# Attention into a MoE layer on one core: batches 3 and 4 turned by the DMA crossbar, attention planned one row chunk later, a fourth buffer of exponentials

## The chip, the cores and the metric

The kernel runs on one core of a Trainium2 chip. The metric is device time in microseconds (us), the median of the runs of a program. One execution of each kernel is profiled as well, and everything that is said of single instructions comes from that execution.

## The reference

```python
# q, k, v: [8 batches, 8 heads, 576 positions, 64] f32
scores = scale * np.matmul(q, k.transpose(0, 1, 3, 2))
scores = np.where(pos[:, None] // 64 >= pos[None, :] // 64, scores, -1e9)
attn = softmax(scores)                                   # over the keys
x = (attn @ v).transpose(0, 2, 1, 3).reshape(8 * 576, 8 * 64)     # 4608 x 512
h = x @ w_in                                             # 4608 x 2048
g = h * (1.0 / (1.0 + np.exp(-beta * h)))
out = g @ w_out                                          # 4608 x 512
```

The attention is causal in blocks of 64 positions. The kernel computes the matmuls in bf16 and gives f32.

## The kernel before

**Attention.** The work is cut into 32 pairs: for each of 8 batches four pairs of heads (u = 4 b + c). For a pair, Q and K are loaded by SyncE (SP), cast to bf16, and turned so that the head dimension lies on the partitions (QKT). In batches 0 and 1 TensorE (PE) turns them (line 561); from batch 2 on (QB = 2) the DMA crossbar does, two pairs at once (line 598). Four groups of score matmuls follow (QK, line 620; they use PE as two halves of 64 rows, one for each head), and for each group ScalarE (ACT) writes the exponentials (lines 628 and 640) into a buffer E; VectorE (DVE) zeroes the masked corners (634, 636). Then 30 matmuls (PV, line 664) multiply the exponentials with V, which carries a column of ones, so that the row sums come with it. DVE takes the reciprocals (676) and scales into xq (683). Last, xq is turned into xT, the transposed attention output: on PE by five transposes for a pair (line 708), copied out of PSUM by DVE or ACT (718, 716), in the batches below XB = 5; by the DMA crossbar from SP (line 696) in the batches from XB on. xT is a ring of 2560 columns; a batch whose 576 columns wrap around its end is moved in three pieces (`pieces`) instead of two, which of all batches is batch 4.

**MoE.** The 4608 rows are cut into 9 chunks of 512. For a chunk, 16 groups of four matmuls (line 752) give h, ACT takes a tanh of each (762), DVE forms the product gT (766), and 64 matmuls (line 785) multiply with w_out; ACT scales the result (797) and issues its store (803). Chunk r needs the attention of the batches that its rows lie in, batch r at the latest. gT has two buffers, one for even and one for odd chunks.

**Order.** All operations are first put into a planner (class `Plan`), which simulates the engines, the buffers and the two DMA rings with given durations, and at each step gives every engine its ready operation with the lowest `prio`. What it yields is the fixed order of every engine's queue; at run time each engine (and the queue of SP, which issues the loads and both kinds of crossbar transposes) goes through its list and waits on semaphores. The numbers that set the order around the change are these:

```python
        LAG = 2
        def pr(u):
            b, c = divmod(u, NPAIR)
            return u if b < 1 else 10 * u if b < 2 else 994 + 100 * (b - LAG) + 4.9 * c
```

QK of a pair has prio `pr(u) + .1` or `+ .2`, PV `pr(u) + .4`, the PE transposes `pr(u) + .5` (5 more for PV and transposes in batch 0), and the MoE of chunk r has `1000 + 100 * r + j` for its 16 groups of h and from `1016 + 100 * r` on for its products with w_out. Exponentials, tanh and most of DVE's work have 0, crossbar transposes -1, loads the number of their pair or batch. Until 50 us of the plan PE gets filling matmuls (469, 471) where it has nothing else.

**Buffers.** E has three buffers (NE = 3), which the pairs take in the order in which they come free. In batch 0 the scores don't wait for a buffer, only the exponentials do. xq has two buffers, QKT three, the raw Q and K six. PSUM has eight banks, of which scores take two pairs and PV one pair.

**Weights.** GpSimd (POOL) casts Q, K and V, and issues the loads of w_in and w_out, in four quarters each (lines 451 and 456). Quarter 1 of w_in has prio -33.2, the casts of V for pairs 2 and 3 of batch 0 have -33, quarters 2 and 3 have -32. Quarters 1 to 3 wait for all of batch 0's V, the w_out quarters for batch 1's V.

Of the kernel before, what the change touches and what calls it, by code (L numbers as in the profile page):

```python
# [4 lines left out]
ACT = mybir.ActivationFunctionType  # L5
ALU = mybir.AluOpType
f32 = mybir.dt.float32
bf16 = mybir.dt.bfloat16
# [7 lines left out]
RC = 512  # L16
NRC = NROWS // RC
NJ = NF // 128
# [320 lines left out]
def bass_blockwise_causal_attn__then__act_swish_beta_kernel(  # L339
# [10 lines left out]
    with es:  # L350
        def sb(name, shape, dt):
            return es.enter_context(nc.sbuf_tensor(name, shape, dt))

        NQ = 2
        QB, XB, CAST = 2, 5, "POOL"
        NE = 3
        NS = 6
        RX = 5 * RC
        ST = [sb(f"ST{i}", [128, 5, 4, 64], f32) for i in range(NS)]
        ST6 = [s[0:96].rearrange("p t h d -> p (t h d)")[:, 0:768].rearrange("p (h j d) -> p h j d", h=2, j=6)  # L360
               for s in ST]
        Vs = [sb(f"Vs{i}", [128, 5, 8, 64], f32) for i in range(NQ)]
        QKn = [sb(f"QKn{i}", [128, 2, 2, 768], bf16) for i in range(NQ)]
        Vn = [sb(f"Vn{i}", [128, 5, 8, 66], bf16) for i in range(NQ)]
        QKT = [sb(f"QKT{i}", [128, 2, 2, 640], bf16) for i in range(3)]
        Ef = [sb(f"E{i}", [128, 3200], bf16) for i in range(NE)]
        E3 = [e[:, 0:3072].rearrange("p (c h n) -> p c h n", c=3, h=2) for e in Ef]
        E4 = [e[:, 3072:3136] for e in Ef]
        inv = [sb(f"inv{i}", [128, 10], f32) for i in range(3)]
        xq = [sb(f"xq{i}", [128, 5, 128], bf16) for i in range(2)]  # L370
# [5 lines left out]
        betaT = sb("betaT", [NJ, 128], f32)  # L376
        beta = sb("beta", [128, NJ], f32)
        th = [sb(f"th{i}", [128, RC], f32) for i in range(3)]
        gT = [sb(f"gT{i}", [128, NJ, RC], bf16) for i in range(2)]
        ost = [sb(f"ost{i}", [128, DM], f32) for i in range(3)]  # L380
        warm = sb("warm", [128, 2], f32)
        PS = es.enter_context(nc.psum_tensor("PS", [128, 8, 512], f32))
# [2 lines left out]
        identW = identF[:].bitcast(bf16)  # L385
        NFILL, TFILL = 400, 50000.0
        P = Plan()
        for c, n in (("ST", NS), ("QKn", NQ), ("V", NQ), ("Vs", NQ), ("QKT", 3), ("E", NE), ("inv", 3), ("xq", 2),
                     ("th", 3), ("gT", 2), ("ost", 3)):
            P.slots(c, n)  # L390

# [6 lines left out]
        def dve_t(n):  # L398
            return (n + 125) / 0.96

        LAG = 2
        def pr(u):
            b, c = divmod(u, NPAIR)
            return u if b < 1 else 10 * u if b < 2 else 994 + 100 * (b - LAG) + 4.9 * c
# [16 lines left out]
        for i in range(NQ):  # L421
# [7 lines left out]
                ones.append(P.op("POOL", 100, mk(lambda g, i=i, h=h: g.memset(  # L429
                    Vn[i][64 * h:64 * h + 64, 4, h:8:2, 64:65], 1.0)), deps=[o], prio=-4))  # L430
            ones.append(P.op("POOL", 100, mk(lambda g, i=i: g.memset(Ef[i][:, 3136:3200], 0.0)), prio=-4))
        for i in range(NQ, NE):
            ones.append(P.op("POOL", 100, mk(lambda g, i=i: g.memset(Ef[i][:, 3136:3200], 0.0)), prio=-4))


# [1 line left out]
                  xfer=100, dma=("d_beta", 1), prio=0.1)  # L437
# [3 lines left out]
                  deps=[bt, c2], tiles=[tb], lat=400, mode="full", prio=5)  # L441
# [5 lines left out]
        win, wout = [], []  # L447
        for a in range(4):
            def fwi(g, e, a=a):
                n = slice(512 * a, 512 * a + 512)  # L450
                return [g.dma_start(w_in[:, :, n], moe_w_in[:, n].rearrange("(c p) n -> p c n", p=128))]

            win.append(P.op("POOL", 1000, fwi, xfer=3150, dma=(f"d_win{a}", 1), prio=-38.5 if a < 1 else -33.2 if a < 2 else -32))
        for a in range(4):
            def fwo(g, e, a=a):
                return [g.dma_start(w_out[:, 4 * a:4 * a + 4, :],
# [6 lines left out]
        for i in range(NFILL):  # L463
# [10 lines left out]
            n = 215 if i < 16 else 110  # L474
# [7 lines left out]
        for b in range(B):  # L482
            ts, t = P.tile("Vs"), P.tile("V")
            tl[b] = t
            for h0, h1 in ([(0, 4), (4, 8)] if b == 0 else [(0, 8)]):
                vs = []
                for i in range(6):
                    def fv(g, e, ts=ts, b=b, h0=h0, h1=h1, i=i):
                        if i < 4:
# [6 lines left out]
                    n = (h1 - h0) / 8 * (1 if i < 4 else 0.25)  # L496
                    vs.append(P.op("SP", 300 + 550 * n, fv, tiles=[ts],
                                   xfer=1580 * n, prio=3.5 + 0.1 * (h0 > 0) if b == 0 else 4 * b + (3.5 if b < 2 else 0.5),
                                   dma=["d_V", h0, 1]))
                ld["V", b, h0] = vs  # L500
                for g0 in range(h0, h1, 2 if b == 0 else 8):
                    g1 = g0 + 2 if b == 0 else h1

                    def fw(g, e, ts=ts, t=t, g0=g0, g1=g1):
# [3 lines left out]
                             prio=4 * b + 0.5 - (38.5 - 5 * (h0 > 0)) * (b < 1))  # L508
# [20 lines left out]
        for u in range(NU):  # L529
            b, c = divmod(u, NPAIR)  # L530
            Tv = tl[b]
            p = c % 2
# [5 lines left out]
            if b < QB:  # L538

                turned = []  # L540
                for w, (nm, src) in enumerate((("Q", q), ("K", k))):
# [9 lines left out]
                    def fn(g, e, ts=ts, tn=tn, p=p, w=w):  # L551
# [5 lines left out]
                             prio=-40 + 3 * u if onp else -1)  # L557

                    def ft(g, e, tn=tn, pt=pt, p=p, w=w):
                        for i in range(6):  # L560
# [5 lines left out]
                             prio=pr(u))  # L566
# [33 lines left out]

                turned = [P.op("SP", 3250, ft, deps=casts, tiles=[tt_, tn], xfer=3200, prio=-1, dma=["d_T", 0, 1])]
            tqk, cps = tt_, turned
            te = P.tile("E")
            ex = []
            zs = []
            for g0 in range(4):
                ps = P.tile("PP" if g0 < 3 else "P1")

                def fq(g, e, ps=ps, g0=g0, tqk=tqk, p=p):
                    blocks = {0: [(0, 0, 512, 0)], 1: [(1, 128, 576, 0), (0, 512, 576, 448)],  # L610
                              2: [(2, 256, 576, 0), (3, 384, 576, 320)], 3: [(4, 512, 576, 0)]}[g0]
                    for t, q0, q1, off in blocks:
                        m = min(128, 576 - 128 * t)
                        for h in range(2):
                            r = slice(64 * h, 64 * h + 64)
                            if g0 < 3:
                                o = PS[0:m, ps.slot + h, off:off + q1 - q0]
                            else:
                                o = PS[r, ps.slot, 0:64]
                            z = g.matmul(o, QKT[tqk.slot][r, p, 1, 128 * t:128 * t + m],  # L620
                                         QKT[tqk.slot][r, p, 0, q0:q1])
                    return z

                o = P.op("PE", 220 if g0 < 3 else 60, fq, deps=cps, tiles=[ps, tqk] + [te] * (b > 0),
                         lat=(220 if g0 < 3 else 60) + 200, mode="row", prio=pr(u) + .1 + .1*(g0 >= 2))
                if g0 < 3:
                    def fe(g, e, ps=ps, g0=g0, te=te):
                        return g.activation(E3[te.slot][:, g0, :, :], PS[:, ps.slot:ps.slot + 2, :], ACT.Exp,  # L628
                                            scale=0.125)
                    x = P.op("ACT", act_t(1024), fe, deps=[o], tiles=[ps, te], lat=act_t(1024) + 93, prio=0)  # L630

                    def fz(g, e, g0=g0, te=te):
                        if g0 < 2:
                            return g.memset(E3[te.slot][64:128, g0, :, 0:64], 0.0)  # L634
                        a = E3[te.slot][64:128, 2, :, 0:64]
                        return g.memset(bass.AP(a.tensor, a.offset, [a.ap[0], [512, 2], [320, 2], [1, 64]]), 0.0)  # L636
                    zs.append(P.op("DVE", 160 if g0 < 2 else 220, fz, deps=[x], tiles=[te], prio=-20))
                else:
                    def fe(g, e, ps=ps, te=te):
                        return g.activation(E4[te.slot][:], PS[:, ps.slot, 0:64], ACT.Exp, scale=0.125)  # L640
                    x = P.op("ACT", act_t(64), fe, deps=[o], tiles=[ps, te], lat=act_t(64) + 93, prio=0)
                ex.append(x)


            def eblk(te, t, i, h):
                if t == 4:
                    a = 3072
                elif t == 0 and i == 4:
                    a = 1024 + 512 * h + 448
                else:  # L650
                    g0, off = {0: (0, 0), 1: (1, 0), 2: (2, 0), 3: (2, 320)}[t]
                    a = 1024 * g0 + 512 * h + off + 128 * i - 128 * t
                return Ef[te.slot][:, a:a + 128]

            pv = P.tile("PP")
            pv.at = (4, 6, 0, 2) if u == 3 else (4, 6) if b < 1 else (0, 2)
# [2 lines left out]
            def fav(g, e, te=te, pv=pv, Tv=Tv, c=c):  # L659
                for h in range(2):  # L660
                    for i in range(5):
# [3 lines left out]
                                         start=(t == 0), stop=(t == i))  # L665
                return z

            av = P.op("PE", 30 * 34, fav, deps=ex + zs + [load[u]], tiles=[te, Tv, pv, ti, tx],
                      lat=30 * 34 + 180, mode="full", prio=pr(u)+.4 + 5 * (b < 1))

# [7 lines left out]
            r = P.op("DVE", 150, fr, deps=[av], tiles=[pv, ti], prio=0)  # L678
# [62 lines left out]
        for r in range(NRC):  # L741
# [5 lines left out]
            for j in range(NJ):  # L747
                ph, tt = P.tile("P1"), P.tile("th")

                def fh(g, e, ph=ph, j=j, row=row):  # L750
                    for c in range(4):
                        z = g.matmul(PS[:, ph.slot, :], w_in[:, c, 128 * j:128 * j + 128], xT[:, c, row % RX:row % RX + RC],  # L752
                                     start=(c == 0), stop=(c == 3))
                    return z

                o = P.op("PE", 4 * mm(512), fh, deps=xd + [win[j // 4]], tiles=[ph, tg], lat=4 * mm(512) + 170,
                         mode="full", prio=1000 + 100 * r + j)

                hs.append(o)

                def fs(g, e, ph=ph, tt=tt, j=j):
                    return g.activation(th[tt.slot][:], PS[:, ph.slot, :], ACT.Tanh, scale=beta[:, j:j + 1])  # L762
                a = P.op("ACT", act_t(512, 1), fs, deps=[o, bC], tiles=[ph, tt], lat=act_t(512, 1) + 93, prio=0)

                def fg(g, e, ph=ph, tt=tt, tg=tg, j=j):
                    return g.scalar_tensor_tensor(out=gT[tg.slot][:, j, :], in0=th[tt.slot][:], scalar=1.0,  # L766
                                                  in1=PS[:, ph.slot, :], op0=ALU.add, op1=ALU.mult)
                gs.append(P.op("DVE", dve_t(512), fg, deps=[a], tiles=[ph, tt, tg], prio=0))

            for b in range(B):  # L770
                if any((S * b + a) // RC - RX // RC == r for a in (0, S - 1)):
# [104 lines left out]
```

## Time and profile before

| What | us |
|---|---|
| median of 6 runs | 354.81 |
| lowest and highest run | 353.75 and 357.78 |
| the profiled execution | 354.25 |
| its span, first to last instruction | 352.4 |
| PE busy with matmuls | 339.4 |
| ACT busy | 212.2 |
| DVE busy | 163.4 |
| first MoE matmul starts | 30.0 |
| PV of the last pair starts | 251.2 |

Busy times are sums over the whole span; a stage's limit is read from the rows of that stage. A group of instructions is named by its line in the code, its engine and what it writes and reads (out<-in); "a <- b: total, times, longest" among the waits means that a was idle until b ended. "PEld" is PE's loading of weights, which runs beside the matmuls. SP isn't counted as busy: its entries are times of issue, in which it holds its queue.

### The profile page before, as it was taken

How to read it: one execution, taken by the hardware profiler on the slowest of the kernel's cores; microseconds unless marked ns; L12 is line 12 of the kernel's file. 1: busy time of each engine (PE TensorE's matmuls, PEld its weight loads, DVE VectorE, ACT ScalarE, POOL GpSimd, SP SyncE). 2: the span in 40 equal slices, each digit the busy share in tenths (PEclk: the TensorE clock that was granted, in tenths of full speed). 3: DMA queues.
4: the chain of work that ended last, by engine and by line, in shares of the span. 5: the costliest groups of instructions: out<-in, count | busy, mean ns of one | idle time of the engine just before them, and what ended most of it. 6: DMA issues, size and time to landing. Idle time of an engine off the chain costs nothing.

```text
span 352.4 us, 6855 instructions
## 1 busy us (share of the span) xinstructions
PE 339.4 (96%) x2767; PEld 171.1 (49%) x2811; DVE 163.4 (46%) x367; ACT 212.2 (60%) x315; POOL 76.3 (22%) x107
## 2 busy tenths in 40 slices
PE   7898999999999999999999999999999999999997
PEld 5475455435455454545444445444444444444444
DVE  3648685038334566127731474127704803712820
ACT  1946963277476897098882977199616715724821
POOL 6376170144044053053012310500000000000000
PEclk9999999999999999999999999999999999999999
DMA  7989999999999999999577886861111011012003
GB/s 204 214 211 252 187 177 199 220 240 218 178 240 208 221 204 201 209 252 196 115 175 161 202 171 144 213 139 36 29 66 60 0 61 60 0 40 80 1 6 115
DMA packets 146672, 52.05 MB, mean 148 GB/s; under 512 B 134720, under 2 KB 142160, under 8 KB 146640
## 3 DMA queue, kind: packets, MB, share of 16 engines
q1 hardware_dynamic: 137088, 37.97, 51.4%
q10 hardware_dynamic: 5328, 9.44, 7.4%
q0 software_dynamic: 4224, 4.19, 7.4%
q8 instruction: 22, 0.36, 0.5%
q14 instruction: 10, 0.08, 0.1%
HBM read 36.71 MB, written 9.44 MB: 131 GB/s over the span
## 4 chain that ended last, share of the span: by engine, by line
PE 90%; DVE 4%; ACT 2%; issue 2%; POOL 0%; POOLq 0%
PE PS L785 36%; PE PS L752 34%; PE PS L620 8%; PE PS L664 7%; PE PS L708 2%; PE PS L469 2%; DVE xq L683 2%; DVE gT L766 1%; PE PS L471 1%; ACT th L762 1%; PE PS L561 1%; ACT E L628 1%; DVE QKT L569 1%; DVE inv L676 0%; ACT xT L716 0%
## 5 line engine op out<-in xcount | busy, mean ns | idle before, releaser
L752 PE MATMUL PS<-xT,w_in 128*128 128x512 bf16 x550 | 129.4, 379 | 3.7 <-issue 1.0
L766 DVE SCALAR_TENSOR_TENSOR gT<-th,PS 128x512 bf16<-128x512 f32 x144 | 97.1, 685 | 75.4 <-ACT th L762 74.4
L785 PE MATMUL PS<-w_out,gT 128*128 128x512 bf16 (+1 forms) x574 | 129.2, 373 | 1.6 <-issue 1.1
L762 ACT ACTIVATE th<-PS,beta 128x512 f32<-128x512 f32 x144 | 98.2, 707 | 25.3 <-PE PS L752 23.3
L628 ACT ACTIVATE E<-PS 128x1024 bf16<-128x1024 f32 x96 | 96.5, 1040 | 24.9 <-PE PS L620 24.7
L785 PEld LDWEIGHTS PS<-w_out,gT 128*128 128x128 bf16 x592 | 55.1, 98 | 63.5 <-issue 4.5
L752 PEld LDWEIGHTS PS<-xT,w_in 128*128 128x128 bf16 x576 | 52.5, 98 | 64.4 <-DVE gT L766 2.6
L797 ACT ACTIVATE ost<-PS 128x512 f32<-128x512 f32 (+1 forms) x37 | 21.7, 589 | 78.9 <-PE PS L785 78.8
L591 POOL CAST QKn<-ST 128x640 bf16<-128x640 f32 x48 | 34.6, 721 | 51.4 <-DMA ST<-in_k_dram 28.8
L620 PE MATMUL PS<-QKT 64*128 64x320 bf16 (+5 forms) x384 | 39.1, 281 | 1.1 <-DVE xq L683 0.5
L505 POOL CAST Vn<-Vs 128x2560 bf16<-128x2560 f32 (+1 forms) x11 | 19.1, 1741 | 84.1 <-DMA Vs<-in_v_dram 84.0
L664 PEld LDWEIGHTS PS<-Vn,E 128*128 128x128 bf16 x960 | 32.5, 97 | 6.8 <-ACT E L640 0.4
L664 PE MATMUL PS<-Vn,E 128*128 128x65 bf16 x960 | 34.1, 193 | 0.5 <-ACT E L640 0.3
L634 DVE MEMSET E<- 64x64 uint32 x64 | 7.1, 112 | 52.4 <-ACT E L628 50.8
L620 PEld LDWEIGHTS PS<-QKT 64*128 64x128 bf16 (+1 forms) x384 | 13.3, 95 | 29.4 <-issue 13.5
L683 DVE TENSOR_TENSOR xq<-PS,inv 128x640 bf16<-128x640 f32 x32 | 26.3, 823 | 0.9
L569 DVE COPY QKT<-PS 128x576 bf16<-128x576 bf16 x16 | 12.0, 756 | 6.5 <-PE PS L561 6.2
L676 DVE RECIPROCAL inv<-PS 128x10 f32<-128x10 f32 x32 | 7.0, 218 | 15.2 <-PE PS L664 15.0
L552 POOL CAST QKn<-ST 96x768 bf16<-96x768 f32 x14 | 11.6, 826 | 6.8 <-DMA ST<-in_k_dram 4.5
L718 DVE COPY xT<-PS 128x64 bf16<-128x64 bf16 (+2 forms) x40 | 9.6, 287 | 6.3 <-PE PS L708 6.1
L636 DVE MEMSET E<- 64x128 uint32 x32 | 5.3, 165 | 14.3 <-ACT E L628 13.3
L708 PE MATMUL PS<-identB,xq 128*128 128x128 bf16 (+1 forms) x100 | 10.5, 216 | 0.4 <-DVE xq L683 0.2
(33 smaller groups left out, 61.6 us busy)
## 6 DMA issues: line engine op xcount, KB each, us to landing
out_dram<-ost ACTq DMA_DIRECT2D x35, 256.0 KB, 2.6
Vs<-in_v_dram SPq DMA_DIRECT2D x28, 256.0 KB, 4.1
ST<-in_q_dram SPq DMA_DIRECT2D x48, 128.0 KB, 3.2
ST<-in_k_dram SPq DMA_DIRECT2D x48, 128.0 KB, 3.2
ST<-in_q_dram SPq DMA_DIRECT2D x8, 288.0 KB, 6.0
ST<-in_k_dram SPq DMA_DIRECT2D x8, 288.0 KB, 7.4
w_in<-in_moe_w_in_dram POOLq DMA_DIRECT2D x4, 512.0 KB, 11.7
w_out<-in_moe_w_out_dram POOLq DMA_DIRECT2D x4, 512.0 KB, 10.3
```

What stands on the lines that cost most here:

```text
L505: return g.tensor_copy(Vn[t.slot][:, :, g0:g1, 0:64], Vs[ts.slot][:, :, g0:g1, :])
L591: return g.tensor_copy(QKn[tn.slot][:].rearrange("p a w n -> p (a w n)")[:, 640 * (2 * a + w):][:, 0:640] .rearrange("p (t h d) -> p t h d ...
L620: z = g.matmul(o, QKT[tqk.slot][r, p, 1, 128 * t:128 * t + m], QKT[tqk.slot][r, p, 0, q0:q1])
L628: return g.activation(E3[te.slot][:, g0, :, :], PS[:, ps.slot:ps.slot + 2, :], ACT.Exp, scale=0.125)
L664: z = g.matmul(o, eblk(te, t, i, h), Vn[Tv.slot][:, t, 2 * c + h, 0:65], start=(t == 0), stop=(t == i))
L683: return g.tensor_tensor(xq[tx.slot][:].rearrange("p i (h d) -> p h i d", h=2), both(pv, 0, 64), x, ALU.mult)
L708: z = g.transpose(PSb[:, px.slot, 128 * i:128 * i + r], xq[tx.slot][0:r, i, :], identB[0:r, 0:r])
L752: z = g.matmul(PS[:, ph.slot, :], w_in[:, c, 128 * j:128 * j + 128], xT[:, c, row % RX:row % RX + RC], start=(c == 0), stop=(c == 3))
L762: return g.activation(th[tt.slot][:], PS[:, ph.slot, :], ACT.Tanh, scale=beta[:, j:j + 1])
L766: return g.scalar_tensor_tensor(out=gT[tg.slot][:, j, :], in0=th[tt.slot][:], scalar=1.0, in1=PS[:, ph.slot, :], op0=ALU.add, op1=ALU.mult)
L785: z = g.matmul(PS[:, po.slot, 0:d1 - d0], gT[tg.slot][:, j, 128 * w:128 * w + 128], w_out[:, j, d0:d1], start=(j == 0), stop=(j == NJ - 1))
L797: return g.activation(ost[to.slot][:, 0:n], PS[:, po.slot, 0:n], ACT.Copy, scale=0.5)
```

## The change

Five things change, of which the last two belong together.

- XB goes from 5 to 3, so the crossbar turns the attention output of batches 3 and 4 too.
- LAG goes from 2 to 1, so attention of batch b (from 2 on) has its place ahead of chunk b-1 instead of chunk b-2.
- Quarter 1 of w_in gets the prio of quarters 2 and 3 (-32).
- Pair 3 (the last one of batch 0) writes its exponentials into an own, fourth buffer, a class "EX" with one slot.
- That buffer lies in gT[1], which chunk 1 is the first to use; the products of chunk 1 therefore get the users of pair 3's exponentials as dependencies. The buffer's padding is zeroed by one more memset on POOL.

```diff
-        QB, XB, CAST = 2, 5, "POOL"
+        QB, XB, CAST = 2, 3, "POOL"
...
         Ef = [sb(f"E{i}", [128, 3200], bf16) for i in range(NE)]
+        gT = [sb(f"gT{i}", [128, NJ, RC], bf16) for i in range(2)]
+
+        Ef.append(gT[1][:].rearrange("p j n -> p (j n)")[:, 0:3200])
...
-        gT = [sb(f"gT{i}", [128, NJ, RC], bf16) for i in range(2)]
...
-        for c, n in (("ST", NS), ("QKn", NQ), ("V", NQ), ("Vs", NQ), ("QKT", 3), ("E", NE), ("inv", 3), ("xq", 2),
+        for c, n in (("ST", NS), ("QKn", NQ), ("V", NQ), ("Vs", NQ), ("QKT", 3), ("E", NE), ("EX", 1), ("inv", 3), ("xq", 2),
...
-        LAG = 2
+        def es_(te):
+            return NE if te.cls == "EX" else te.slot
+
+        LAG = 1
...
-        for i in range(NQ, NE):
+        for i in range(NQ, NE + 1):
...
-            win.append(P.op("POOL", 1000, fwi, xfer=3150, dma=(f"d_win{a}", 1), prio=-38.5 if a < 1 else -33.2 if a < 2 else -32))
+            win.append(P.op("POOL", 1000, fwi, xfer=3150, dma=(f"d_win{a}", 1), prio=-38.5 if a < 1 else -32))
...
-            te = P.tile("E")
+            te = P.tile("EX" if u == 3 else "E")
...
+            if u == 3:
+                spare = te
...
-                gs.append(P.op("DVE", dve_t(512), fg, deps=[a], tiles=[ph, tt, tg], prio=0))
+                gs.append(P.op("DVE", dve_t(512), fg, deps=[a] + (spare.users if r == 1 else []), tiles=[ph, tt, tg], prio=0))
```

Where the code picked a buffer of exponentials by `te.slot`, it now does by `es_(te)`.

More of the change, by code (lines that the diff above doesn't have):

```diff
@@ L627, in fe @@
                     def fe(g, e, ps=ps, g0=g0, te=te):
-                        return g.activation(E3[te.slot][:, g0, :, :], PS[:, ps.slot:ps.slot + 2, :], ACT.Exp,
+                        return g.activation(E3[es_(te)][:, g0, :, :], PS[:, ps.slot:ps.slot + 2, :], ACT.Exp,
                                             scale=0.125)
@@ L633, in fz @@
                         if g0 < 2:
-                            return g.memset(E3[te.slot][64:128, g0, :, 0:64], 0.0)
-                        a = E3[te.slot][64:128, 2, :, 0:64]
+                            return g.memset(E3[es_(te)][64:128, g0, :, 0:64], 0.0)
+                        a = E3[es_(te)][64:128, 2, :, 0:64]
                         return g.memset(bass.AP(a.tensor, a.offset, [a.ap[0], [512, 2], [320, 2], [1, 64]]), 0.0)
@@ L639, in fe @@
                     def fe(g, e, ps=ps, te=te):
-                        return g.activation(E4[te.slot][:], PS[:, ps.slot, 0:64], ACT.Exp, scale=0.125)
+                        return g.activation(E4[es_(te)][:], PS[:, ps.slot, 0:64], ACT.Exp, scale=0.125)
                     x = P.op("ACT", act_t(64), fe, deps=[o], tiles=[ps, te], lat=act_t(64) + 93, prio=0)
@@ L652, in eblk @@
                     a = 1024 * g0 + 512 * h + off + 128 * i - 128 * t
-                return Ef[te.slot][:, a:a + 128]
+                return Ef[es_(te)][:, a:a + 128]
             pv = P.tile("PP")
```

## The prediction, made before the changed kernel was run

> **What bounds the kernel now.** I read the busy shares, the 40 slices and the chain that ended last first, to see which engine sets the time:
>
> ```profile
> span 352.4 us, 6855 instructions
> PE 339.4 (96%) x2767; PEld 171.1 (49%) x2811; DVE 163.4 (46%) x367; ACT 212.2 (60%) x315; POOL 76.3 (22%) x107
> ...
> PE   7898999999999999999999999999999999999997
> ...
> ACT  1946963277476897098882977199616715724821
> ...
> DMA  7989999999999999999577886861111011012003
> ...
> PE 90%; DVE 4%; ACT 2%; issue 2%; POOL 0%; POOLq 0%
> ```
>
> TensorE (PE) is full in every slice but the first four, and 90% of the chain is PE. A busy PE need not be PE at its pace, but in the pure MoE stretches a 128x512 matmul takes 0.216 us (46 of them in 9.93 us of the chain), and the stretches with attention keep that pace between attention pieces. So from about 30 us on the kernel is PE work laid end to end: what leaves PE leaves the time, and before 30 us it is the latency to the first MoE matmul that counts. DMA is full until about 165 us (slice 19), then half idle.
>
> For the start I read the waits and the timeline from 21 to 31 us:
>
> ```profile
> ACT E L640 <- PE PS L664: 3.7, 1, 3.7
> ...
> 21.34 0.74 POOL L451 DMA_DIRECT2D w_in<-in_moe_w_in_dram  x1 [0.94 <-DMA Vs<-in_v_dram]
> 22.08 1.52 POOL L505 CAST Vn<-Vs 128x640 bf16<-128x640 f32 x2
> 22.27 2.85 ACT L628 ACTIVATE E<-PS 128x1024 bf16<-128x1024 f32 x3
> 25.14 2.15 PE L664 MATMUL PS<-Vn,E 128*128 128x65 bf16 x60
> 30.03 0.81 PE L752 MATMUL PS<-xT,w_in 128*128 128x512 bf16 x3 [0.42 <-ACT xT L716]
> ```
>
> The exponentials of pair 3 stand on ACT for 3.7 us until PV of pair 0 gives its E buffer back (three buffers, four pairs). They run at 22.27 to 25.1; PV of pairs 2 and 3 then runs together at 25.14, and the first MoE matmul follows at 30.03. Also, POOL issues quarter 1 of w_in at 21.34, ahead of the casts of V for pairs 2 and 3.
>
> For the transposes, the queue of SyncE (SP) and ACT's load I read the groups, SP's waits, SP's timeline and the windows:
>
> ```profile
> L718 DVE COPY xT<-PS 128x64 bf16<-128x64 bf16 (+2 forms) x40 | 9.6, 287 | 6.3 <-PE PS L708 6.1
> ...
> L708 PE MATMUL PS<-identB,xq 128*128 128x128 bf16 (+1 forms) x100 | 10.5, 216 | 0.4 <-DVE xq L683 0.2
> ```
> ```profile
> PEld PS L620 <- issue: 13.5, 43, 0.4
> ...
> SPq L696 <- DVE gT L766: 19.1, 7, 7.2
> ...
> 167.84 3.27 SPq L696 DMA_TRANSPOSE xT<-xq  x2
> ...
> 120.00:130.00 10.00, 9.15 (x90) 4.60 (x92) 6.51 (x17) 9.60 (x18) 3.76 (x3) 1.00 0.98 201
> 167.80:171.10 3.30, 3.30 (x18) 1.32 (x18) 1.78 (x6) 3.30 (x6) 0.00 (x0) 1.00 0.24 50
> 230.00:240.00 10.00, 9.68 (x86) 4.64 (x86) 4.60 (x13) 9.98 (x17) 0.00 (x0) 1.00 0.55 120
> 240.00:250.00 10.00, 9.79 (x107) 4.85 (x108) 7.40 (x17) 9.41 (x14) 0.00 (x0) 1.00 0.22 45
> ```
>
> 100 transpose matmuls are 20 pairs (batches 0 to 4) of five. In the window rows the columns are PE, weight loads, DVE, ACT, POOL, clock, DMA share and GB/s: with two crossbar transposes on SP (167.8 to 171.1) DMA falls to 50 GB/s, since nothing else is issued meanwhile.
>
> [...] Here five on PE are pipelined into 0.34 to 0.66 us; a crossbar piece holds SP for 1.23 us and lands 2.5 us after issue. [...] SP stands up to 7.2 us for a crossbar whose input isn't there, with the loads behind it. [...] 43 QK weight loads (64-row mode) waited 13.5 us, 0.31 each.
>
> **The change part by part.**
>
> *Crossbar from batch 3 (XB 5 to 3).* Removed: the PE transposes of pairs 12 to 19. From the weight-load starts, to what follows: 0.66, 0.66, 0.35, 0.34, 0.46, 0.66, 0.34, 0.46 = 3.93 us. Pairs 15 and 18 sit between two QK bursts, so removing them saves a drain of 0.31 each; at pair 14 a following QK burst would drain anyhow (-0.12): 3.93 + 0.62 - 0.12 = 4.4 us of PE. Bounds 3.7 (chain pieces of 0.46 x 8) and 4.9. Also removed: 20 DVE copies at 9.6/40 = 0.24, 4.8 us, nothing, as DVE is 46% busy. Added: 20 crossbar DMAs on SP (2 for each pair of batch 3, 3 in batch 4 where the ring of xT wraps), 20 x 1.25 = 25 us of SP. Each stands in SP's queue until its xq is made, and the loads of batches 5 to 7 are behind it. From SP's timeline a batch costs Q and K 4 x 2.9, V 3.6, two QKT crossbars 7.6 = 22.8 us, plus 8 x 1.25 = 10 (15 in batch 4): 33 to 38 us, against some 37 us of PE for a chunk with attention (27.6 + 9.4). I take nothing, because of the next part.
>
> *LAG 2 to 1.* Attention of batch b is due before chunk b-1 instead of b-2; chunk b needs it. It removes and adds no instruction. In the trace the early batches ran later than LAG 2 asks anyway, since loads were late: PV of batch 3 at 109 to 132, of batch 4 at 136 to 162 (chunk 3 from 152, chunk 4 from 196). So batches 5 to 7 move most. Loads: the second QKT of batch 5 lands at 168; plus 25 us is 193. With chunk 4 at about 190 and chunk 5 at about 225, the two pairs behind it end near 193 + 12 = 205: 20 us to spare. ACT: 16 tanh x 0.71 + 4 pairs x 3.3 = 24.5 us against PE 13.8 + 9.4 = 23.2 when all four pairs fall into one h stretch; batch 7 does that today (230 to 250), and PE is 9.68 and 9.79 of 10. So 0; bounds -1.5 (the stall at 120 to 130 goes) and +5 (rival 2).
>
> *Own exponentials for pair 3, and w_in quarter 1 later.* The exponentials of pair 3 move from 22.27 into ACT's gap at 18.4 to 22, ending near 21.7. The casts of V for pairs 2 and 3 start at 21.34 instead of 22.08, so pair 2 can start at 22.2. Then PV: pair 0 at 21.03, 1 at 22.05, 2 at 23.3 (it needs the bank that pair 0's scaling, ending 23.2, frees), 3 at 24.3 to 25.4. Reciprocal and scaling 0.22 + 0.82: 26.45; transposes 0.5; ACT copies 0.71: 27.7; first MoE matmul at 28.0, not 30.0: 2.0 us. Bounds 0 and 3.7 (the whole wait). Chunk 0 then runs 2 us earlier. Behind it come V of batch 1 (cast done 47.0; PV at 49.5 would be 47.5), w_out quarters 0 to 3 (landed 52.2, 55.9, 59.3, 62.6; first used 55.0, 59.1, then about 62 and 65, would be 53, 57.1, 60, 63): each just clears. Quarter 1 of w_in is issued 1.5 us later, landing near 33.4; its first use at about 37.5 becomes 35.5. One POOL memset of 0.15 is hidden in POOL's 0.27 us wait for the first K (else 0.15 of start). The new waits of chunk 1's DVE products on pair 3's users are long met (26 against 69 us).
>
> *Sum.* 352.4 - 4.4 - 2.0 + 0 = 346.0. The profiled run took 354.25, 1.85 outside the span: 347.85; the median of the runs is 0.56 over that run: 348.4.
>
> **The rivals.**
>
> 1. *The start's gain stops at the next wall.* Chunk 0 ends early and PE then stands for V of batch 1 or a quarter of w_out, whose times DMA sets (share over 1 from 50 to 70). For: margins of 0.4 to 1.2 us. Against: each still clears. All 2.0 back: 350.4.
> 2. *LAG costs PE.* All of a batch's exponentials meet the tanh in one h stretch, and batches 3 to 7 each lose what 120 to 130 loses (0.85): 4.3 us, 352.7; or 14 more QK bursts at 0.31, about the same. Against: batch 7 today.
> 3. *SP becomes the bound (slower).* The crossbars' waits on SP stand before the loads in the stretch where DMA is full. Today's 12 crossbar pairs wait 25.4 us in all (19.1 + 3.8 + 2.5), 2.1 each; eight more are 17 us, with the 25 us of issue 42 us. That decides once the load delay passes 25 + 20 = 45 us in batch 5, or batches 6 and 7 pile up another 15: PE then stands at a chunk's start for what is over. With 57 us of delay 12 us are lost: 360. For: 33 to 38 us of SP a batch against 37. Against: SP waits only when it is ahead, and DMA is half idle after 165 us.
> 4. *More than the sum*: the stalls of 111 to 140 (1.3 us) go and the start gains 3: 346.
>
> **How the numbers follow.** Forecast 0.56 (348.4, own range 346.5 to 350.5), rival 1 0.16, rival 2 0.13, rival 3 0.09, rival 4 0.06. About 1% is what a measurement can tell from no change: faster is under 351.3, slower over 358.4. Faster: 0.56 + 0.06 + 0.11 of rival 1 = 0.73; same: the rest of rival 1 and 0.12 of rival 2 = 0.17; slower 0.10. The range 345.5 to 353.5 leaves out rival 3 and the edges of 2 and 4, about 0.17.
>
> **What would show it.** The L708 row falls to x60 and SP's L696 calls rise to 44; the wait of L640 on L664 is gone and the first L752 matmul starts at 28; PE waits at 47 to 66 us don't grow. PE busy falls by about 6 us with its share unchanged; attention ends near 285 instead of 255. I am wrong on the start if PV of pair 1 or w_out is waited for, and on SP if PE shows gaps of microseconds ahead of L620 or at a chunk's first L752 after 140 us.

## The result and the profile after

The changed kernel takes 358.47 us (median of 21 runs, 355.64 to 364.1) where the kernel before takes 354.60 in the runs taken beside it (42): the ratio is 1.0088, with a 95% interval of 1.0065 to 1.011. It is slower by 3 to 4 us (the ratio makes 3.1, the two medians are 3.9 apart); I had forecast 6 us less. The profiled execution took 357.58 us, and the line numbers of the new kernel are 5 to 7 higher (QK is 625, PV 669, the PE transposes 715, the crossbar of xT 703, h 759, the products with w_out 792).

The page of the changed kernel, the same rows as before:

```profile
span 355.8 us, 6784 instructions
PE 337.2 (95%) x2733; PEld 169.1 (48%) x2776; DVE 157.9 (44%) x347; ACT 209.3 (59%) x315; POOL 76.5 (21%) x108
...
PE   7899999999999999999899999798999999999996
...
ACT  1945973278467791699039943886169814823831
...
DMA  8999999989999885985479987994650221002003
...
PE 77%; DVE 6%; ACT 6%; SPq 4%; DMA 3%; issue 2%; POOL 0%; ACTq 0%; POOLq 0%
```

The matmuls did shrink, but PE has dents now, in slices 20, 26 and 28 of 40 (8, 7 and 8 tenths), and the chain has a share for SP's queue (4%) and for DMA (3%), which it had not. The transposes went as planned, by the groups (count, busy us, mean ns):

```profile
L715 PE MATMUL PS<-identB,xq 128*128 128x128 bf16 (+1 forms) x60 | 6.3, 216 | 0.3 <-DVE xq L690 0.3
```

What PE and SP wait for (us in total, times, longest), by the waits of the changed kernel; before, PE had no wait for a DMA in this list at all:

```profile
PE PS L669 <- DMA xT<-xq: 2.8, 2, 1.4
PE PS L625 <- DMA QKT<-QKn: 2.6, 1, 2.6
...
SPq L703 <- DVE gT L773: 25.3, 7, 10.9
...
SPq L703 <- DVE xq L690: 7.4, 5, 2.7
SPq L703 <- DVE E L641: 1.7, 1, 1.7
...
SPq L703 <- DVE E L639: 1.4, 2, 0.9
```

The three places on PE's timeline, and the windows of 10 us around them (columns as in the prediction):

```profile
169.93 1.06 PE L669 MATMUL PS<-Vn,E 128*128 128x65 bf16 x30 [1.43 <-DMA xT<-xq]
...
231.03 0.22 PE L625 MATMUL PS<-QKT 64*64 64x64 bf16 x2 [2.62 <-DMA QKT<-QKn]
...
245.09 1.06 PE L669 MATMUL PS<-Vn,E 128*128 128x65 bf16 x30 [1.37 <-DMA xT<-xq]
```
```profile
120.00:130.00 10.00, 9.84 (x103) 5.08 (x103) 6.22 (x14) 8.40 (x15) 0.00 (x0) 1.00 0.78 141
160.00:170.00 10.00, 8.52 (x74) 3.79 (x74) 7.00 (x15) 8.74 (x14) 2.32 (x1) 1.00 0.49 90
220.00:230.00 10.00, 8.25 (x78) 3.95 (x78) 4.14 (x12) 9.26 (x14) 3.71 (x6) 1.00 1.02 231
240.00:250.00 10.00, 8.53 (x92) 4.54 (x93) 6.42 (x13) 5.64 (x9) 2.32 (x1) 1.00 0.48 104
```

QK at 231 waits for its turned Q and K, which the crossbar brings late. PV at 170 and 245 has its data, but no xq buffer for the scaling that follows: there are two, and on the crossbar path a buffer is free only when its crossbar transfer has landed (2.5 us after issue in the median of 44, 4.4 at most), and the two waits of 1.43 and 1.37 us end with such a landing. The old stall at 120 to 130 (9.15 of 10) is gone: 9.84.

Behind these waits stands SP. Its timeline in the changed kernel where the new crossbars begin:

```profile
117.40 2.46 SPq L703 DMA_TRANSPOSE xT<-xq  x2
119.91 3.60 SPq L603 DMA_TRANSPOSE QKT<-QKn  x1
123.56 2.54 SPq L703 DMA_TRANSPOSE xT<-xq  x2
126.14 1.21 SPq L495 DMA_DIRECT2D Vs<-in_v_dram  x2
127.39 1.28 SPq L498 DMA_DIRECT2D Vs<-in_v_dram  x2
128.71 2.25 SPq L585 DMA_DIRECT2D ST<-in_q_dram  x4
```
```profile
122.38 2.26 SPq L580 DMA_DIRECT2D ST<-in_q_dram  x4
```

The second fence is the kernel before: the same load of Q starts at 122.38, so it is 6.3 us late behind the first four crossbars, which hold SP for 5.0 us. From 117.4 to 260 us no two groups on SP's timeline are more than 0.3 us apart. The waits view puts 24.4 us of this stretch down to inputs that a crossbar stood for, but they lie inside the issues, most of which are of ordinary length: the 36 pieces of xT and 8 QKT crossbars of the stretch take together 11.8 us more than if each were as short as the shortest of its kind, so at most that is waiting. SP issues for 136.7 of the 142.6 us, while the DMA engines are busy for 0.81 of them: its queue is the limit here, and what is late stays late. The landings of the second QKT of batches 4 to 7: 142.0, 167.8, 205.5, 237.4 us before; 150.7, 194.6, 231.0, 261.9 after. The delay is 9, 27, 25 and 24 us, and the crossbars hold SP for 20 x 1.244 = 24.9 us. It isn't the lag's doing: with LAG = 1 and no added crossbar (e4 below) the four landings are 142.8, 170.5, 203.1 and 237.6, within 3 us of before.

**Where the 3.3 us of span come from** (352.44 to 355.77). I cut both traces at three starts on PE.

| stretch | before | after | difference |
|---|---|---|---|
| to the first PV | 21.03 | 21.69 | +0.7 |
| to the first h matmul | 9.00 | 9.11 | +0.1 |
| to the first product with w_out | 24.94 | 25.75 | +0.8 |
| to the end | 297.47 | 299.22 | +1.8 |

The first row is scatter of single executions: with the start of the kernel before, the first PV lies anywhere from 20.08 to 21.96 in the traces of e1, e2, e9, e10, e11, e13 and e14 below, and in e3, with the new start, at 20.41. The third row is the new start's own cost, as e3 and e4 have it too (25.75 and 25.74) and e2 and e9 don't (24.92 and 24.93): in the new order h waits for a DVE copy of turned Q and K, which it did not before.

```profile
38.11 0.81 PE L759 MATMUL PS<-xT,w_in 128*128 128x512 bf16 x3 [0.85 <-DVE QKT L574]
```

The last row is the crossbar's part. I sum the time from each kind of weight load on PE to the next kind, from the first h matmul to the end: the PE transposes fall from 8.07 to 4.46, -3.6 us, and the waits for DMA add 5.4 (2.8 + 2.6), together +1.8.

### The profile page after: what moved, and what is told of

The parts are those of the page before. It is cut to its first block, busy times and chain, and to the rows that moved or that the text cites. A ratio compares the mean times of both kernels' runs of the same rounds, so it can differ in the third digit from the quotient of the medians.

```text
span 355.8 us, 6784 instructions
## 1 busy us (share of the span) xinstructions
PE 337.2 (95%) x2733; PEld 169.1 (48%) x2776; DVE 157.9 (44%) x347; ACT 209.3 (59%) x315; POOL 76.5 (21%) x108
## 4 chain that ended last, share of the span: by engine, by line
PE 77%; DVE 6%; ACT 6%; SPq 4%; DMA 3%; issue 2%; POOL 0%; ACTq 0%; POOLq 0%
PE PS L792 32%; PE PS L759 29%; PE PS L669 6%; PE PS L625 6%; ACT th L769 3%; ACT E L633 3%; SPq L703 2%; PE PS L474 2%; DVE QKT L574 2%; SPq L585 2%; DVE xq L690 2%; DMA QKT<-QKn 1%; DVE gT L773 1%; DMA xT<-xq 1%; PE PS L476 1%
## 5 line engine op out<-in xcount | busy, mean ns | idle before, releaser
L759 PE MATMUL PS<-xT,w_in 128*128 128x512 bf16 x552 | 131.4, 380 | 3.2 <-issue 1.0
L792 PE MATMUL PS<-w_out,gT 128*128 128x512 bf16 (+1 forms) x573 | 126.9, 373 | 1.4 <-issue 0.6
L633 ACT ACTIVATE E<-PS 128x1024 bf16<-128x1024 f32 x93 | 94.7, 1046 | 19.3 <-PE PS L625 19.1
L792 PEld LDWEIGHTS PS<-w_out,gT 128*128 128x128 bf16 x592 | 56.2, 98 | 64.2 <-issue 2.6
L759 PEld LDWEIGHTS PS<-xT,w_in 128*128 128x128 bf16 x576 | 51.6, 98 | 62.5 <-issue 5.1
L625 PE MATMUL PS<-QKT 64*64 64x64 bf16 (+5 forms) x384 | 38.6, 281 | 3.7 <-DMA QKT<-QKn 2.6
L669 PEld LDWEIGHTS PS<-Vn,E 128*128 128x128 bf16 x930 | 31.4, 97 | 10.5 <-DVE gT L773 3.7
L669 PE MATMUL PS<-Vn,E 128*128 128x65 bf16 x930 | 32.8, 193 | 3.4 <-DMA xT<-xq 2.8
L625 PEld LDWEIGHTS PS<-QKT 64*128 64x128 bf16 (+1 forms) x384 | 13.3, 95 | 34.5 <-issue 13.6
L474 PE MATMUL PS<-identF,identB 128*128 128x256 bf16 x51 | 9.1, 328 | 3.6 <-POOL identF L415 2.4
L645 ACT ACTIVATE E<-PS 128x64 bf16<-128x64 f32 x31 | 6.7, 251 | 2.8 <-PE PS L625 2.8
```

The source lines that it names most:

```text
L633: return g.activation(E3[es_(te)][:, g0, :, :], PS[:, ps.slot:ps.slot + 2, :], ACT.Exp, scale=0.125)
L669: z = g.matmul(o, eblk(te, t, i, h), Vn[Tv.slot][:, t, 2 * c + h, 0:65], start=(t == 0), stop=(t == i))
L792: z = g.matmul(PS[:, po.slot, 0:d1 - d0], gT[tg.slot][:, j, 128 * w:128 * w + 128], w_out[:, j, d0:d1], start=(j == 0), stop=(j == NJ - 1))
```

## The experiments

All ratios are to the kernel before, with 95% intervals. First, the three parts by themselves.

**e1_crossbar_only**: the kernel before with

```diff
-        QB, XB, CAST = 2, 5, "POOL"
+        QB, XB, CAST = 2, 3, "POOL"
```

> The kernel before with XB = 3 alone (attention as early as before, no own buffer for pair 3). Theory S (SP is the cause: 20 more crossbar transposes hold the loads and the two xq buffers behind them in SP's order, and TensorE waits): slower than before by 1 to 8 us, with TensorE waits of over 1 us ahead of QK or PV from 150 us on that the kernel before lacks. Rival L (planning attention one chunk later is the cause, the crossbar is free): faster by about 4 us, the 4.4 us of transposes that leave TensorE.

Measured: 363.44 us, 1.0264 (1.0211 to 1.0316). That is a little more than the 8 us that I had allowed. The crossbar alone is worse than the whole change: PE waits 8.5 us for turned Q and K (4 times) and 2.1 for exponentials.

**e2_lag_only**: the kernel before with

```diff
-        LAG = 2
+        LAG = 1
```

> The kernel before with LAG = 1 alone. Theory S: within 1.5 us of before, no TensorE wait of over 1 us after 60 us. Rival L: slower by 2 to 5 us, with the loss spread over the stretches where h and attention share ScalarE.

Measured: 354.81 us, 0.9995 (0.9966 to 1.0024). The lag costs nothing and gives nothing, and PE waits for no DMA. So it matters only as room: the two edits together must be compared with each alone.

**e3_start_only**: the changed kernel with XB = 5 and LAG = 2, so only the own buffer and the order of w_in remain.

```diff
-        QB, XB, CAST = 2, 3, "POOL"
+        QB, XB, CAST = 2, 5, "POOL"
...
-        LAG = 1
+        LAG = 2
```

> The kernel before with the own buffer for pair 3 and the later w_in quarter alone. In the changed kernel the first MoE matmul starts at 30.8 instead of 30.0 us: if that is this part's doing, it starts near 30.8 here too and the time is 0 to 1 us over before. If the start's loss came from something else, it starts at or before 30.0 and the time is 0 to 2 us under before.

Measured: 355.17 us, 1.0028 (1.0002 to 1.0053): about 1 us lost instead of 2 gained. Neither branch of the expectation holds: the first h matmul starts at 29.52, ahead of 30.03, and the time is over all the same. The loss is the 0.8 us between h and the products with w_out, shown above.

**e4_all_but_crossbar**: the changed kernel with XB = 5.

> The changed kernel with XB back at 5. Theory S: the TensorE waits at 168, 228 and 243 us (5.3 us together) are gone and the eight pairs of transposes (4.4 us) are back: 1 to 3 us under the changed kernel, within 1.5 us of before. Rival L: as slow as the changed kernel or slower (358 to 363).

Measured: 356.13 us, 1.0032 (1.0007 to 1.0056). From here to the changed kernel, 358.47, the crossbar of batches 3 and 4 costs 2.3 us, where I had forecast 4.4 saved.

Next, four tries to take the wait away.

**e5_three_xq**: the changed kernel with three xq buffers.

```diff
-        xq = [sb(f"xq{i}", [128, 5, 128], bf16) for i in range(2)]
+        xq = [sb(f"xq{i}", [128, 5, 128], bf16) for i in range(3)]
```

> The changed kernel with three xq buffers instead of two. Theory S in two parts: PV of a pair can't start until the crossbar has emptied an xq buffer (waits at 168 and 243 us, 2.9 us), and the QKT of batch 6 comes late through SP (228 us, 2.5 us). This takes away the first part alone: about 355.5, PE's waits on xT<-xq gone, the wait on QKT left at 2 to 4 us. If only the lateness of the loads counts, the time stays within 1 us of the changed kernel and the wait on QKT grows by what was saved.

Measured: 358.33 us, 1.009 (1.0063 to 1.0117). PE's waits in it:

```profile
PE PS L625 <- DMA QKT<-QKn: 5.5, 3, 2.6
```

The waits for xq (2.8) are gone, and those for QKT have grown from 2.6 to 5.5: the sum, 5.5 against 5.4, is the same. A third buffer moves the wait and doesn't take it away.

**e6_v_loads_on_pool** and **e7_v_on_pool_three_xq**: V of batches 2 on is issued by POOL instead of SP; the second has three xq buffers as well.

```diff
-                    vs.append(P.op("SP", 300 + 550 * n, fv, tiles=[ts],
+                    vs.append(P.op("SP" if b < 2 else "POOL", 300 + 550 * n if b < 2 else 1000, fv, tiles=[ts],
```

> The changed kernel with the loads of V from batch 2 on issued by GpSimd instead of SP: 36 issues, some 22 us, leave SP's queue; nothing else changes. Theory S (SP's queue is the bound): the waits on QKT and on xT<-xq shrink to under 1.5 us together, 353 to 356. If the 16 DMA engines and not the queue are the bound, the waits stay and the time stays within 1 us of the changed kernel.

> Both of the above. Theory S: no TensorE wait of over 1 us after 60 us; the 4.4 us of transposes now come out of the time: 351 to 353.5, under the kernel before. If TensorE loses elsewhere when attention comes later, 354 or more with no such waits left.

Measured: 365.82 us, 1.031 (1.0216 to 1.0404), and 370.72 us, 1.0416 (1.0337 to 1.0495). Both are no test of SP alone: POOL's casts of Q and K now stand behind its issues of V, and SP waits for them at the QKT crossbar, 21.2 us (longest 5.1) in the first, where it was 16.5 in the changed kernel. Two QKT crossbars together hold SP for 11.1 to 12.8 us there (three times, at 84.88, 111.72 and 149.41), where none of the changed kernel holds it for over 5.0. What of the time this costs isn't separated. In the second PE waits 13.7 us for xT. So these two don't test whether SP's queue or the 16 DMA engines are the limit; for the queue speaks the trace of the changed kernel above, and no experiment.

**e8_crossbar_after_loads**: the changed kernel with the crossbars behind the loads.

```diff
-                xt.append(P.op("SP", 1300 * n, fy, deps=nrm, tiles=[tx], xfer=1100, prio=-1,
+                xt.append(P.op("SP", 1300 * n, fy, deps=nrm, tiles=[tx], xfer=1100, prio=40,
```

> The changed kernel with the crossbar transposes of the attention output behind the loads in the planner's order of SP (prio 40 instead of -1). It trades one hold for the other: the wait on QKT goes (2.5 us less), the PV waits for an xq buffer grow. Slower than the changed kernel by 1 to 8 us if the two xq buffers are the tighter limit, faster by up to 2.5 us if the loads are.

Measured: 378.08 us, 1.0646 (1.0593 to 1.0699), far over the 8 us expected at most. Late crossbars are worse than late loads: PE waits 3.3 us for xq and 9.1 for exponentials in all, and in its trace the granted clock is 0.50 for 27.3 us (149.1 to 155.9, 193.5 to 207.2, 244.7 to 251.5); PE is busy for 18.2 us of it, so that by my estimate up to half of these, 9.1 us, of the loss come with the lower clock.

Then the crossbar with the lag, without the start, and how much of it pays.

**e9_no_own_buffer**: the kernel before with XB = 3 and LAG = 1.

> XB = 3 and LAG = 1 without the own buffer for pair 3 and the moved w_in quarter. If the parts add up, about 1 us under the changed kernel: 357.4; the TensorE waits of the crossbar (some 5 us from 150 us on) stay.

Measured: 357.64 us, 1.0072 (1.005 to 1.0093). Against the crossbar alone (363.44) the lag takes back 5.8 us; against the lag alone (354.81) the crossbar costs 2.8.

**e10_batch3_only**: the kernel before with LAG = 1 and

```diff
-            if b >= XB:
+            if b == 3 or b > 4:
```

> As e9, but of batches 3 and 4 only batch 3 is turned by the crossbar: 8 crossbar transposes (10 us of SP) instead of 20 (25 us). Theory S (loads come late by what the crossbars hold SP): the loads of batches 5 and 6 come 8 to 12 us later than in the kernel with LAG = 1 alone, within what LAG = 1 gave them; no TensorE wait of over 1 us, four pairs of transposes (2.2 us) leave TensorE: 352 to 353.5. If a crossbar costs by itself and not by the delay, half of what e9 loses: 355.5 to 356.5.

Measured: **352.88 us, 0.9942 (0.9918 to 0.9966)**, faster than both kernels. Eight crossbars instead of twenty, and PE's waits for DMA are one line:

```profile
PE PS L664 <- DMA xT<-xq: 0.9, 1, 0.9
```

PE transposes take 2.7 us less than with the lag alone (6.58 against 9.30); less the 0.9 of waiting, 1.8 us should be left, and 1.9 is measured.

**e11_planner_told**: e9 with the QKT crossbar planned at 4.2 us on SP instead of 3.25.

```diff
-                turned = [P.op("SP", 3250, ft, deps=casts, tiles=[tt_, tn], xfer=3200, prio=-1, dma=["d_T", 0, 1])]
+                turned = [P.op("SP", 4200, ft, deps=casts, tiles=[tt_, tn], xfer=3200, prio=-1, dma=["d_T", 0, 1])]
```

> As e9, but the planner counts 4.2 us instead of 3.25 for a QKT crossbar on SP (the chip takes 3.6 to 4.2), so that TensorE's order expects QKT as late as it comes. If the waits are only TensorE's fixed order, with other work ready behind, they go: 1.5 to 3 us under e9. If SP's queue is the bound, the waits only move: within 1.5 us of e9.

Measured: 356.32 us, 1.0041 (1.0018 to 1.0064), 1.3 us better than e9. PE still waits 2.1 us for QKT, 1.7 for xq and 1.4 for the products: an order that counts more for the crossbar moves the waits, it makes no room on SP.

**e12_pv_banks**: e3 with other PSUM banks allowed to pair 2's PV.

```diff
-            pv.at = (4, 6, 0, 2) if u == 3 else (4, 6) if b < 1 else (0, 2)
+            pv.at = (4, 6, 0, 2) if u in (2, 3) else (4, 6) if b < 1 else (0, 2)
```

> e3 (the start's part alone) with one more change: PV of pair 2 may take PSUM banks 0 to 3 too, as PV of pair 3 may. If PSUM banks, not the exponentials, held the start (in e3 PV of pair 2 waits until pair 1 is scaled, 3.25 us after PV of pair 0 began), the first MoE matmul comes 7.2 to 8.0 us after the first PV instead of 8.85, and the time is 0.8 to 1.6 us under e3: 353.6 to 354.4. If not, 8.85 and 355.2 stay.

Measured: 353.92 us, 0.9983 (0.9961 to 1.0005), 1.25 us better than e3, as expected, but the first h matmul comes 8.69 us after the first PV and not 7.2 to 8.0. It is read in the next section.

Last, dose and lag apart.

**e13_batch3_lag2**: e10 with LAG = 2. **e14_batch4_only**: the kernel before with LAG = 1 and XB = 4, so batch 4 alone is added. **e15_paying_parts**: the changed kernel with e10's condition and e12's banks.

> The kernel before (LAG = 2) with batch 3 turned by the crossbar too, batch 4 not: 8 more crossbars, 10 us of SP. If the delay counts against the room of LAG: 10 us without the extra room, so TensorE waits of 1 us or more on QKT or xT<-xq appear, 355 to 359, between before and e1 (363.4), and over e10 (352.9) by 2 us or more. If each crossbar costs as such, as at LAG = 1: 352.5 to 353.5, as e10.

> As e10, but batch 4 alone goes through the crossbar instead of batch 3 alone: 12 crossbars, 15 us of SP. By the delay: a little more than e10, still near what LAG = 1 has room for: 352.5 to 354.5. If the three-piece transfers of batch 4 are what hurts in the changed kernel, nearly its whole loss is here: 356 or more.

> The changed kernel with batch 4 turned by TensorE again (crossbar for batch 3 and from 5 on) and PV of pair 2 allowed PSUM banks 0 to 3: the parts that paid in e10 (-1.6 us against before) and e12 (-0.5). If they add up: 352.0 to 352.8, under both kernels.

Measured: 362.27 us, 1.0189 (1.0143 to 1.0234); 358.51 us, 1.0123 (1.0065 to 1.0181); 354.96 us, 1.0006 (0.9977 to 1.0035). PE's waits of e13 and of e14:

```profile
PE PS L620 <- DMA QKT<-QKn: 7.7, 3, 4.9
PE PS L664 <- DMA xT<-xq: 1.5, 1, 1.5
```
```profile
PE PS L664 <- DMA xT<-xq: 4.2, 2, 2.4
PE PS L752 <- DMA xT<-xq: 1.4, 1, 1.4
```

The eight crossbars of batch 3 that gain 1.9 us at LAG 1 lose 7.9 at LAG 2 (362.27 against 354.4, the kernel before in the same runs): the same work on SP, 10 us, and only the room differs. That is more than I expected (355 to 359), and in part it may be the clock: it is 0.50 from 248.8 to 255.6 us, at and after the wait of 4.9, and half of the 4.6 us behind that wait (PE goes on at 251.02) is 2.3 us, by estimate. The miss of e14 matters more. By the delay alone I expected 352.5 to 354.5, and 356 or more if the three-piece transfers of batch 4 are what hurts; it came at 358.51. Twelve crossbars of batch 4 make PE wait as long (5.6 us) as twenty of both batches (5.4), all of it for xT<-xq. So the cost doesn't grow by the piece, and SP's total isn't the whole of it; whether it is batch 4's third piece or its place in the order, no run separates. e15 did not add up either: in its profile PE waits 0.2 us for a DMA and the span is 351.9, but its runs spread from 352.5 to 357.2.

**The account.** To the time with LAG 1 and no added crossbar (354.8 without the own buffer, 356.1 with it) I add PE's waits for DMA and take off what the PE transposes fell by in the trace:

| kernel | transposes | waits | account, us | measured, us |
|---|---|---|---|---|
| e10, batch 3 | -2.7 | 0.9 | 353.0 | 352.88 |
| e14, batch 4 | -2.3 | 5.6 | 358.1 | 358.51 |
| e9, both | -4.8 | 4.4 | 354.4 | 357.64 |
| the changed kernel | -4.8 | 5.4 | 356.7 | 358.47 |

Two close; e9 and the changed kernel are 3.2 and 1.8 us over. In e9 the trace shows what is over, in the wait and in three windows cut at the edges of its slow stretch:

```profile
229.78 0.26 PE L620 MATMUL PS<-QKT 64*64 64x64 bf16 x2 [2.75 <-DMA QKT<-QKn]
```
```profile
210.00:229.00 19.00, 16.87 (x118) 7.68 (x117) 4.50 (x13) 11.03 (x17) 5.99 (x9) 1.00 0.95 201
229.00:236.20 7.20, 6.09 (x43) 3.15 (x45) 1.95 (x5) 2.51 (x4) 0.00 (x0) 0.53 1.07 173
236.20:250.00 13.80, 13.64 (x123) 6.45 (x125) 9.50 (x20) 10.31 (x15) 3.01 (x2) 1.00 0.63 133
```

PE stands for QKT until 229.8; the granted clock is 0.53 from 229.0 to 236.2, and for the 6.4 us of it behind the wait I estimate up to 6.4 x 0.47 = 3.0 us on top. The length of the gap doesn't say in these traces whether the clock falls: after 2.75 us it did here and after 2.61 in e5 (0.50 for 3.4 us), while the changed kernel kept 1.00 after 2.62 us and e1 after 3.24. First e5, then e1:

```profile
232.38 0.22 PE L625 MATMUL PS<-QKT 64*64 64x64 bf16 x2 [2.61 <-DMA QKT<-QKn]
...
233.60:237.00 3.40, 3.40 (x32) 1.79 (x31) 1.37 (x2) 2.29 (x3) 0.00 (x0) 0.50 1.43 187
```
```profile
237.55 0.22 PE L620 MATMUL PS<-QKT 64*64 64x64 bf16 x2 [3.24 <-DMA QKT<-QKn]
...
237.60:245.00 7.40, 7.08 (x91) 4.06 (x94) 4.84 (x11) 5.36 (x9) 1.37 (x1) 1.00 1.00 213
```

In the changed kernel 17 of 22 runs have a mean clock of 0.995 or less, against 44 of 129 of the kernel before; 0.005 of 357 is 1.8 us. That its other runs lose the clock after the same gap would fit, as it happened in e5's trace, but they have no trace; and a low mean can come from elsewhere, for in the traces of e4, e10, e12 and e13 the clock is 0.50 for 3.4 to 6.8 us between 12 and 19 us, at the start (their means over the whole run are 0.99, 0.995, 0.995 and 0.986, that of e13 with the stretch from 248.8 in it). So it isn't shown. The runs with a mean clock of 1.00 bound it: their medians are 354.1 us (before, 76 runs), 357.6 (the changed kernel, 5), 355.7 (e9, 6), 352.2 (e10, 4) and 357.8 (e14, 3). The change thus loses 3.5 us where no clock is lost, and the clock is not the reason that it is slower; of e9's 3.2 us some 2 go with it.

## Why the prediction was wrong, point by point

**The PE transposes (-4.4): right.** 60 matmuls are left, and the time on PE fell by 3.6 us (against the kernel before) or 4.8 us (against e4, the same kernel without the crossbars). What the forecast calls a drain is the idle time of 0.31 us that the trace before shows ahead of QK's weight loads (13.5 us in 43); that two of them would go with the transposes was an estimate, and the new trace doesn't show it (13.6 us in 44).

**SP's 25 us hidden by the lag (0): wrong, and this decides.** The sizes of issue and delay were right: 20 x 1.244 us of issue; 27 us of delay for batch 5 where I had 25; the second QKT of batch 5 at 194.6 for 193. The wait at the xT crossbars grew from 25.4 to 35.8 us, not by 17; and 16.7 us of the 25.4, the 7.2 us wait among them, come after 233 us, when no load stands behind it any more (21.6 of the 35.8 after 260), so I had read too much into them. What failed is the step "20 us to spare": I measured the slack to the deadline, the chunk that needs the batch, and let PE do other work until then. PE's queue is a fixed order. Each QK and PV has its place in it among the matmuls of an earlier chunk, and a transfer that misses this place stops everything behind it, however far the chunk is. Batch 5 met its place, with 2.9 us to spare and not 20 (its second QKT landed at 194.6, QK stood at 197.5); batch 6, as late, missed it by 2.6 us at 228.4, though chunk 6, the first to need it, began only at 262.3. The second half of the step failed too: I took DMA's idle half after 165 us for room in which the loads catch up. The queue that issues them had no gap from 117 to 260 us, and the delay stayed at 24 to 27 us. (It can shrink: with the eight crossbars of e10 it is 16 us in batch 5 and 8 in batch 7, against e2.) And I left out that the crossbar changes who frees an xq buffer: a landing on the DMA side, 2.5 us after issue, instead of five matmuls on PE; this is half of the wait (2.8 us). In e5, with a third buffer, the same sum of waiting stands at QKT instead.

**Rival 3 (SP becomes the bound) had the right mechanism and the wrong threshold.** I let it decide from 45 us of delay on and cost 12 us; it decided at 25, and cost 5.4 us on PE. Without the lag it is lower still: in e13 10 us of issue cost more than 7. With it, e14 says that there is no single threshold in SP's total: 15 us of batch 4 cost 4, 10 us of batch 3 gained.

**The lag (0): right by itself** (e2), and rival 2 fell: the stall at 120 to 130 went (9.15 to 9.84), with no new one in its place. Its worth in the change is the room that it makes for late loads: 5.8 us between e1 and e9.

**The start (-2.0): wrong, by the step "PV of pair 2 at 23.3".** The wait of ACT did go; the exponentials of pair 3 follow without a gap in the changed kernel (ACT, then PE):

```profile
15.55 3.29 ACT L633 ACTIVATE E<-PS 128x1024 bf16<-128x1024 f32 x3
18.74 0.22 ACT L645 ACTIVATE gT<-PS 128x64 bf16<-128x64 f32 x1
```
```profile
21.69 1.99 PE L669 MATMUL PS<-Vn,E 128*128 128x65 bf16 x60
...
24.94 1.08 PE L669 MATMUL PS<-Vn,E 128*128 128x65 bf16 x30 [0.46 <-DVE xq L690]
...
26.30 1.08 PE L669 MATMUL PS<-Vn,gT 128*128 128x65 bf16 x30
...
30.80 0.81 PE L759 MATMUL PS<-xT,w_in 128*128 128x512 bf16 x3
```

From the first PV to the first h matmul it is 9.11 us, and it was 9.00 (30.03 - 21.03); I had 6.97. PV of pair 2 comes 3.25 us after the first PV instead of 2.27, since it waits for a second scaling on DVE and not for pair 0's; pair 3's comes 4.61 after it instead of 3.27; and from there it is 4.50 us to h, where I had 3.7. So ACT's 3.7 us had stood beside the chain PV, scaling, transposes, copies, and not in it. The trace before has this already: of the 60 PV matmuls from 25.14 on the first 30 are pair 2's, so those of pair 3 begin near 26.2, 1.1 us after its exponentials had ended. And behind h the new order loses the 0.8 us of the stretch table, a term that the sum did not have. e12 lets pair 2 have another bank: it starts 2.72 us after the first PV (24.83 - 22.11), and h 8.69 us after it. That pair 2 stood for a bank is thus shown, for 0.5 of the 2.1 us; the rest is only placed. Most of e12's 1.25 us isn't at the start: from the first product with w_out to the end its trace takes 296.09 us and e3's 297.44, and I have no cause for that.

**Rival 1** (the gain lost at the next wall) didn't come to a test, as there was no gain; what PE stood for behind h was neither V nor w_out but a copy on DVE. What stays open: 1 to 2 us of the changed kernel over the account, what makes batch 4 dearer than batch 3, and why e15's parts didn't add up in the median.

## What to carry to other kernels

Where engines run a fixed order, measure slack to the place at which the consumer stands in its queue, not to the deadline behind it; and before calling an added transfer hidden, count the issue time of its queue over the whole stretch: a queue without gaps can keep a delay to its end (24 to 27 us here, up to 260 us). When a step moves from an engine to a DMA, ask which buffers are now freed by the landing (here 2.5 us after issue). Move work to such a queue in parts and measure each, for the eight pieces of batch 3 paid here (352.88 us), while the twelve of batch 4 (358.51) and all twenty cost.

## What the runs showed of the hardware

In some of these traces PE ran at a lower granted clock after a wait, and the length of the wait didn't decide it. The clock stood at about half after gaps of 2.61 us (e5, 0.50 for 3.4 us) and 2.75 us (e9, 0.53 from 229.0 to 236.2), and stayed at 1.00 after 2.62 us (the changed kernel, 1.00 from 231.03 to 240) and after 2.99 and 3.24 us (e1, mean of the run 1.00). In e7 (mean 0.981) the h matmuls right behind the waits of 4.68 and 8.98 us take 0.45 to 0.47 us each (1.89 us for 4, 3.59 for 8), where groups of 4 and 8 later in the same trace take 1.04 and 1.90 us (at 238.53 and 211.32).
